# Attention and soft experts in one program: the last key tile in contiguous halves, and a sixth chunk of weights loaded at the first heads

## The chip, the cores and the metric

The kernel runs on one core of one Trainium2 chip. The metric is the device time of one execution in microseconds (us), from its start to its end on that core. The times shown for a kernel are a median over several executions; the profile is of one further execution, whose own time is given beside its span.

## The reference

Two stages, one behind the other. The first is attention within clusters: every query and key goes to the nearest of 16 centroids, and a query sees only the keys of its own cluster.

```python
q_assign = np.argmax(np.einsum('bhsd,hcd->bhsc', q_n, c_n), axis=-1)
k_assign = np.argmax(np.einsum('bhsd,hcd->bhsc', k_n, c_n), axis=-1)
mask = q_assign[:, :, :, None] == k_assign[:, :, None, :]
scores = scale * np.matmul(q, k.transpose(0, 1, 3, 2))
scores = np.where(mask, scores, -1000000000.0)
scores = scores - np.max(scores, axis=-1, keepdims=True)
attn = np.exp(scores)
attn = attn / (np.sum(attn, axis=-1, keepdims=True) + 1e-09)
x = np.matmul(attn, v)        # B=4, H=8, S=768, D=64, float32
```

The second is a soft mixture of 8 experts with 4 slots each over all 3072 rows (4 x 768) of the 512 columns that the heads make together. The dispatch weights are a softmax over the rows, the combine weights one over the 32 slots, of the same logits.

```python
logits = x @ phi                                  # 3072 x 32
d = softmax(logits, axis=0)
slot_input = (d.T @ x).reshape(E, S_per_e, D)     # 8 x 4 x 512
slot_out[e] = np.maximum(slot_input[e] @ w1[e], 0.0) @ w2[e]   # 512 -> 1024 -> 512
c = softmax(logits, axis=1)
out = c @ slot_out                                # 3072 x 512
```

The experts' weights are 16 MB each for `w1` and `w2`, 32 MB together.

## The kernel before

**Heads.** The program goes through 32 heads (4 batches of 8) one after the other, overlapped. A head's queries and keys come transposed from memory in one load (`qkT`, 384 KB), its values in another (`vt`). They are split into a high and a low part for precision (`split_hi`, L601, a cast; `split_lo`, L604, a subtraction on GpSimd); for the first two heads the casts are on ScalarE, then in turn on GpSimd and ScalarE. Copies from SBUF to SBUF (`dma`, L358, from the helpers `place1`, `place2` and so on) put the parts, the one-hot rows of the clusters and the row maxima into the operands of the score matmuls: 96 or 192 KB each, nine or ten for a head. All DMAs go through SyncE's queue. Eight lanes (completion counters) are given to the DMAs in turn: a DMA is issued only when the one eight before it, which had the same lane, is complete.

A head's scores are made twice: `pass_a` (L648) for the row maxima, which VectorE takes (`rowmax`, L656), and `pass_b` (L692), keys by queries, for the exponentials. There are 6 key tiles of 128 keys. For each tile ScalarE makes two exponentials out of PSUM (`expo`, L708), a high part in half precision and the whole in float32; `elow` (L712) subtracts the one from the other for a low part; `pass_c` (L729) multiplies both with the values. A string tells which engine subtracts for each of the 6 tiles, P for GpSimd and D for VectorE (`LOWS`, and `LAST_LOWS` for the last head); with D the whole exponential stays in the PSUM bank of the scores, with P it goes to SBUF. `norm` (L743 to L745) divides by the sums, `xtrans` (L754) and `xtrans_out` (L759) transpose two heads' output together, and `logits` (L766, L778) multiplies with `phi`.

**Order.** `Plan` puts the operations of every engine into one fixed order, from due times in a table `K` and estimated durations. What an engine is to do is therefore a list, and it waits at an instruction whose inputs are not there.

**The last head.** Its last key tile (tile 5) is worked in two halves, u=0 and u=1, so that the first half of the output can be normalised while the second is in work. A half is every second block of 128 queries: `part` takes blocks 0, 2, 4 or 1, 3, 5 of one bank, so that both halves wait for all four matmuls of `pass_b`. Between them stand dummy matmuls without a reader (`fill`, `unread`, L934), 5, 7 and 1 of them about this place.

**Behind the last head.** Dispatch weights (`disp`), their transposes (`dtrans`, L803 and L806), the sum of rows by slot in two parts (`slotin`, L833), their scaling (`fin3`, L914; `fin4`, L918). The combine logits of the last batch are transposed (`comb`, the same lines L803 and L806) after `fin3` of the second part; `comb1` to `comb3` make the softmax. Then the experts: `ffn1` (L1222), `relu`, `ffn1_t` (L1250), `ffn2` (L1264) by three column parts, `sums`, `slots` (L1278), and `combine` (L1298, L1305), whose results leave in ten outputs of 512 KB.

**Weights.** They are 16 chunks of 2 MB: 0 to 7 of `w1`, 8 to 11 and 12 to 15 of `w2`. `NPRE` = 5 chunks have buffers of their own and are loaded in 40 pieces of 256 KB beside the heads from head 2 on (`load_w`, L1149). Seven more go into room that the heads' buffers leave, each piece when its room is free, and four (`used`, `BUF`) into buffers whose weights have been used in the experts.

The program begins with dummy matmuls (`warm`, L1185) that stand between the first real ones. `mask_out` (L584) writes the one-hot mask rows of a head into its operands: for the first half (u=0) of the queries (k=0) and the keys (k=1) on ScalarE, for the other on VectorE; for the second head one call covers all.

## Time and profile before

| | before |
|---|---|
| median of 3 runs | 469.69 us (468.64 to 470.2) |
| the profiled execution | 468.94 us |
| its span in the profile | 465.5 us |
| TensorE busy (PE) | 450.0 us, 97% |
| VectorE busy (DVE) | 365.1 us, 78% |
| ScalarE busy (ACT) | 367.4 us, 79% |
| GpSimd busy (POOL) | 314.2 us, 67% |
| moved by DMA | 103.67 MB, mean 223 GB/s |

Times in the profile count from the start of the span. PE is TensorE's matmuls, PEld its weight loads, SPq the DMA queue of SyncE as its issuing engine. The page cuts the span in 40 slices of 11.6 us; a digit is a busy share in tenths. A line of a timeline has start, duration, engine, line of the kernel, operation, output and inputs by their buffers' names, and in square brackets how long the engine had been idle and what ended that. The chain of waits is followed back from the last instruction, and gives for each moment the work that set the end. In a table of stretches every engine has its busy time in that stretch and its count of instructions; then come TensorE's granted clock (1.00 is full), the mean busy share of the 16 DMA engines and what they moved.

### The profile page before, as it was taken

Reading aid. Unit: us, or ns where it says so; the run is one execution under the profiler, and the core shown is the slowest. Engines: PE = TensorE matmul, PEld = TensorE weight load, DVE = VectorE, ACT = ScalarE, POOL = GpSimd, SP = SyncE. Lnnn points to the kernel's source line nnn. Section 1 sums busy time; section 2 is a strip of 40 time slices with the busy share of each in tenths; the row PEclk is TensorE's granted clock in tenths of the full one; section 3 lists DMA queues with packets and bytes.
Section 4 is the critical chain, followed back from the end, with each engine's and each line's share of the span. In section 5 each row is a group of like instructions: output and inputs, shape, how many; then the busy total and the mean of one; then the engine's idle time right before and its main releaser. Section 6 shows DMA issues by size and latency. Waiting matters only on the chain.

```text
span 465.5 us, 15360 instructions
## 1 busy us (share of the span) xinstructions
PE 450.0 (97%) x6139; PEld 362.5 (78%) x6139; DVE 365.1 (78%) x728; ACT 367.4 (79%) x572; POOL 314.2 (67%) x245
## 2 busy tenths in 40 slices
PE   8999999999999999999999999999999999999993
PEld 7777887979797788888886888787868888753572
DVE  6999898989898889898988888888899875362243
ACT  6379999999998798989895989898969989810042
POOL 8358888888888678787876787878775887501000
PEclk9999999999999999999999999999999999999998
DMA  8945876787777676788676578867854778999997
GB/s 241 227 127 145 223 212 174 213 220 213 188 199 208 177 196 180 195 226 219 186 205 184 143 202 222 222 172 205 222 154 128 203 191 242 341 413 408 408 381 293
DMA packets 43035, 103.67 MB, mean 223 GB/s; under 512 B 7834, under 2 KB 12372, under 8 KB 42964
## 3 DMA queue, kind: packets, MB, share of 16 engines
q1 hardware_dynamic: 42964, 102.69, 75.6%
q8 instruction: 48, 0.79, 0.8%
q14 instruction: 23, 0.19, 0.1%
HBM read 52.63 MB, written 6.29 MB: 127 GB/s over the span
## 4 chain that ended last, share of the span: by engine, by line
PE 88%; DVE 4%; ACT 3%; issue 1%; DMA 1%; POOL 0%; SPq 0%; DVEq 0%; POOLq 0%
PE pb L692 29%; PE pc L729 22%; PE pa L648 16%; PE pso L1264 3%; PE ph L1222 3%; PE pt L483 3%; PE pt L754 2%; ACT w L708 2%; PE pt L766 1%; PE po L1298 1%; PE pt L495 1%; PE pc L1185 1%; PE pt L530 1%; DMA w<-vt 1%; PE pt L667 1%
## 5 line engine op out<-in xcount | busy, mean ns | idle before, releaser
L708 ACT ACTIVATE w<-pb 128x768 f16<-128x768 f32 (+2 forms) x320 | 241.7, 814 | 36.9 <-PE pb L692 34.4
L712 POOL TENSOR_TENSOR w<-w,w 128x768 f16<-128x768 f32 x127 | 209.4, 1657 | 76.7 <-ACT w L708 52.2
L656 DVE TENSOR_REDUCE mc<-pa 128x1 f32<-128x512 f32 (+1 forms) x288 | 188.5, 685 | 28.2 <-PE pa L648 26.5
L692 PE MATMUL pb<-w 128*128 128x512 f32 (+1 forms) x576 | 152.1, 350 | 2.0 <-DVE w L712 1.4
L729 PE MATMUL pc<-vx,w 128*128 128x65 f16 x3402 | 132.0, 194 | 0.6 <-POOL w L712 0.3
L729 PEld LDWEIGHTS <-w 128*128 128x128 f16 x3456 | 116.2, 97 | 13.2 <-issue 8.6
L692 PEld LDWEIGHTS pb<-w 128*128 128x128 f32 x576 | 102.4, 188 | 23.3 <-DVE w L712 4.4
L648 PE MATMUL pa<-w 128*128 128x256 f32 (+1 forms) x384 | 112.8, 368 | 0.4 <-ACT w L584 0.3
L712 DVE TENSOR_TENSOR w<-pb,w 128x768 f16<-128x768 f32 (+1 forms) x66 | 62.0, 940 | 18.1 <-ACT pb L708 14.8
L648 PEld LDWEIGHTS pa<-w 128*128 128x128 f32 x384 | 62.2, 189 | 16.3 <-DVE mc L656 13.0
L604 POOL TENSOR_TENSOR w<-w,w 128x768 fp32r<-128x768 f32 x32 | 58.7, 1834 | 5.4 <-ACT w L601 4.1
L692 PE MATMUL pb<-w,w 128*128 128x512 f32 x192 | 60.3, 337 | 0.0
L708 ACT ACTIVATE pb<-pb 128x768 f32<-128x768 f32 (+1 forms) x66 | 53.6, 812 | 0.0
L692 PEld LDWEIGHTS pb<-w,w 128*128 128x128 f32 x192 | 36.2, 188 | 5.1
L636 POOL TENSOR_TENSOR vx<-w,vx 128x384 f16<-128x384 f32 x32 | 28.7, 895 | 1.2 <-ACT vx L632 1.1
L745 DVE TENSOR_TENSOR w<-pc,z 128x384 f32<-128x384 f32 (+1 forms) x32 | 17.7, 552 | 1.1
L628 ACT ACTIVATE w<-w 128x384 f32<-128x384 f32 x32 | 17.1, 533 | 1.8 <-DMA w<-vt 1.8
L601 POOL CAST w<-w 128x768 fp32r<-128x768 f32 x15 | 12.4, 826 | 8.9 <-DMA w<-w 8.9
L632 ACT CAST vx<-w 128x384 f16<-128x384 f32 x32 | 17.2, 538 | 0.1
L533 ACT ACTIVATE w<-pt,ohsc 128x768 fp32r<-128x768 bf16 x15 | 13.7, 915 | 3.2 <-DVE mc L656 3.2
L754 PE MATMUL pt<-ident,w 128*128 128x128 f32 x90 | 15.8, 285 | 0.0
L1264 PE MATMUL pso<-w,hT 128*32 128x128 f32 (+1 forms) x384 | 15.7, 310 | 0.0
(162 smaller groups left out, 380.2 us busy)
## 6 DMA issues: line engine op xcount, KB each, us to landing
w<-w SPq DMA_DIRECT2D x128, 192.0 KB
w<-w SPq DMA_DIRECT2D x188, 96.0 KB
w<-qkT SPq DMA_DIRECT2D x32, 384.0 KB
w<-w1r SPq DMA_DIRECT2D x40, 256.0 KB
w<-w2b SPq DMA_DIRECT2D x16, 512.0 KB
w<-w2a SPq DMA_DIRECT2D x13, 512.0 KB
w<-vt SPq DMA_DIRECT2D x32, 192.0 KB
out<-w SPq DMA_DIRECT2D x10, 512.0 KB
```

The lines of the kernel that those rows point to most:

```text
L604: nc.gpsimd.tensor_sub(RL[i % 2], R[i % 3], RH[i % 2].bitcast(F32))
L632: (nc.scalar.copy if e == "ACT" else ENG[e].tensor_copy)(VXs[i % 2][:, :, D:2 * D], V[i % 2])
L636: nc.gpsimd.tensor_sub(vx[:, :, 0:D], V[i % 2], vx[:, :, D:2 * D])
L648: nc.tensor.matmul(pa[:, c0:c0 + w], q1[:, q0:q0 + P], k1[:, k0:k0 + w], start=True, stop=True)
L656: nc.vector.tensor_reduce(hd[i]["mc"][:, 4 * m + c0:4 * m + c1], pa.rearrange("p (n c) -> p n c", n=c1 - c0), axis=AX.X, op=ALU.max, negat ...
L692: nc.tensor.matmul(pbt[j % 2][:, q0:q1], k_[:, kc], q_[:, q0:q1], start=(o == 0), stop=(o == 1))
L708: nc.scalar.activation(part(dst, u), part(pbt[j % 2][:, 0:S], u), AF.Exp, scale=SCALE)
L712: (nc.vector if lows(i)[j] == "D" else nc.gpsimd).tensor_tensor(part(EL[n % NEL], u), part(e32(i, j), u), part(EH[n // 2 % (NEH // 2)][:, ...
L729: nc.tensor.matmul(pc[:, c0:c0 + w], e[:, ts], vx[:, j, r0:r0 + w], start=(j == 0 and c0 == 0 and o == 0), stop=(j == NT - 1 and o == 2), ...
L745: nc.vector.tensor_tensor(xn, pv[:, :, :, 0:D], z.unsqueeze(3).to_broadcast([P, 2 if u is None else 1, NU, D]), op=ALU.mult)
L754: nc.tensor.transpose(out=pv[:, a, 0:P] if a < 2 else pv[:, :, P:QS], in_=XN[p % 5][:, u + 2 * a, :], identity=ident)
L1264: nc.tensor.matmul(pso[32 * g:32 * g + 32, 0:w], hT[:, r, ff, g, :], chunk(10 + 2 * q + r if q else 8 + 2 * r + c, (fs * g + f) * w, w), s ...
```

## The change

**A sixth chunk at the first heads.** `NPRE` is 6. The 40 pieces on SyncE's queue still cover chunks 0 to 4, at the same heads; chunk 5 is loaded in four pieces of 512 KB on ScalarE's queue, two behind the key half of `mask_out` of head 0 and two behind that of head 1. Only three chunks (13 to 15) go into used buffers. Room comes from small tiles (`mx`, `m2`, `mc`, `nm`, `z`) that now lie in `siT`, from the mask `em`, now in `acc`, and from a smaller scratch area of the program.

**The last key tile.** `pass_b` of tile 5 is made in two halves, each with two matmuls into a bank of its own. Half 0 is queries 0 to 383 as they lie, with the blocks 0, 2, 4 gathered beforehand in the operand view; on it ScalarE makes one exponential in place, VectorE casts it for the high part and subtracts; on half 1 ScalarE makes two exponentials and VectorE subtracts. The subtraction of tile 4 is moved from GpSimd to VectorE. The dummies are 3, 3 and 1, into another bank. The second transposed copy (`xtrans_out`, u=1) is on ScalarE.

**Combine weights.** The transposes of the last batch's combine logits take the place of 5 dummies before the last part of the dispatch; `comb1` waits for `fin4`. `fin4` of the first part is on ScalarE. In the experts, `ct_rest` comes after the first sums and its copy after `slots`; two calls of `ffn2` are cut at other places, so that the first `combine` stands earlier.

```diff
-LAST_LOWS = "PDPDPD"
+LAST_LOWS = "PDPDDD"
...
-    NPRE = 5
+    NPRE = 6
...
         if u == 0:
             nc.scalar.mul(o, ps, -BIG if k else 1.0)
+            if k == 1:
+                for h in range(2):
+                    load_w(NPRE - 1, (2 * i + h) * CW // 4, CW // 4, nc.scalar)
...
+    def half(u):
+        return pbt[1][:, 512 * u:512 * u + HS].rearrange("p (a c) -> p a c", c=P)
+
+    def pass_b_half(i, j, u):
+        for o, (q_, k_) in enumerate((q1k1(i), q2k2(i))):
+            nc.tensor.matmul(half(u), k_[:, j * P:(j + 1) * P], part(q_, u), start=(o == 0), stop=(o == 1))
...
+    def expo_half(i, j, u):
+        if u == 1:
+            nc.scalar.activation(seg(ehigh(i, j), u), half(u), AF.Exp, scale=SCALE)
+        nc.scalar.activation(half(u), half(u), AF.Exp, scale=SCALE)
+
+    def ehigh_half(i, j, u):
+        nc.vector.tensor_copy(seg(ehigh(i, j), u), half(u))
+
+    def elow_half(i, j, u):
+        nc.vector.tensor_tensor(seg(EL[(NT * i + j) % NEL], u), half(u), seg(ehigh(i, j), u), op=ALU.subtract)
...
-        (nc.scalar.copy if apool(p) is None else nc.vector.tensor_copy)(pr[p]["xT", u], pr[p][u][:, 0:HS])
+        (nc.scalar.copy if apool(p) is None or u == 1 else nc.vector.tensor_copy)(pr[p]["xT", u], pr[p][u][:, 0:HS])
...
         if last:
-            fill("B", 5, [("d4", b)])
+            combs("fill", [("ls", b), ("d4", b), ("ct", 1)])
...
-        nc.vector.tensor_copy(siT[:, ca:cb, :].rearrange("p c s -> p (c s)"), mg["ps", ca][:, 0:(cb - ca) * NS])
+        (nc.vector.tensor_copy if ca else nc.scalar.copy)(
+            siT[:, ca:cb, :].rearrange("p c s -> p (c s)"), mg["ps", ca][:, 0:(cb - ca) * NS])
...
-    em = tail.tile([P, 2, 4, NS], F32, name="em")
+    em = acc[:, 0:2 * 4 * NS].rearrange("p (r g s) -> p r g s", r=2, g=4)
...
-    BUF = list(range(NW)) + [0, 3, 4, 5]
+    BUF = list(range(NW)) + [0, 3, 4]
...
-        m = {0: 12, 3: 13, 4: 14, 5: 15}.get(n)
+        m = {0: 13, 3: 14, 4: 15}.get(n)
```

Below, rows of the order of an engine's instructions: line, operation, output and inputs, and what each waits for (DMAHW with a number is a lane; PE, DVE, Activation and Pool are the other engines). Lines of the changed kernel stand 9 to 51 further down than before.

On ScalarE, from the masks of head 0 to the cast of head 2: L584 is `mask_out` and L601 the cast. Before:

```order
L584 ACTIVATE w_0_88<-pb_124 32x384 [waits PE_49]
L584 ACTIVATE w_0_88<-pb_124 32x384
L490 COPY w_86<-pt 128x384 [waits PE_49]
L584 ACTIVATE w_0_91<-pt 32x768 [waits PE_49]
L584 ACTIVATE w_0_91<-pt 32x768
L601 CAST w_87<-w_86 128x768 [waits DMAHW4_49,DMAHW6_49,DMAHW3_49,DMAHW7_49,DMAHW0_49,Pool_49]
```

In the changed kernel, where they are L593 and L613, and L1197 is `load_w`:

```order
L593 ACTIVATE w_0_89<-pb_122 32x384 [waits PE_49]
L593 ACTIVATE w_0_89<-pb_122 32x384
L1197 DMA w_86<-w1r 128x1024
L1197 DMA w_86<-w1r 128x1024 [waits DMAHW6_49]
L499 COPY w_87<-pt 128x384 [waits PE_49]
L593 ACTIVATE w_0_92<-pt 32x768 [waits PE_49]
L593 ACTIVATE w_0_92<-pt 32x768
L1197 DMA w_86<-w1r 128x1024 [waits DMAHW4_49]
L1197 DMA w_86<-w1r 128x1024 [waits DMAHW6_49]
L613 CAST w_88<-w_87 128x768 [waits DMAHW1_49,DMAHW7_49,DMAHW0_49,Pool_49]
```

The four loads stand behind the masks of heads 0 and 1. They have the lanes 3, 6, 4 and 6; the second waits for an earlier copy of lane 6, the fourth for the second load.

On SyncE's queue, from the values of a head (`vt`) over the place copies of head 1 (`w_0_91`) to those of head 2 (`w_1_92`, `w_1_89`). Before:

```order
L475 DMA w_94<-vt 128x384 [waits DMAHW0_49,Pool_49]
L358 DMA w_0_91<-w_87 64x768 [waits DMAHW1_49]
L358 DMA w_0_91<-w_87 64x768 [waits DMAHW2_49]
L475 DMA w_94<-vt 128x384 [waits DMAHW3_49,Pool_49]
L358 DMA w_0_91<-w_87 32x768 [waits DMAHW4_49]
L358 DMA w_0_91<-w_87 32x768 [waits DMAHW5_49]
L472 DMA w_86<-qkT 128x768 [waits DMAHW6_49,PE_49]
L358 DMA w_1_92<-w_87 64x768 [waits DMAHW7_49]
L358 DMA w_1_89<-w_87 64x768 [waits DMAHW0_49,Activation_49]
L358 DMA w_1_89<-w_87 64x768 [waits DMAHW1_49]
L358 DMA w_1_89<-w_87 32x768 [waits DMAHW2_49]
L358 DMA w_1_89<-w_87 32x768 [waits DMAHW3_49,Pool_49]
```

In the changed kernel, where L367 is the copy and the operands are `w_0_92`, `w_1_93` and `w_1_90`:

```order
L484 DMA w_95<-vt 128x384 [waits DMAHW2_49,Pool_49]
L367 DMA w_0_92<-w_88 64x768 [waits DMAHW3_49]
L367 DMA w_0_92<-w_88 64x768 [waits DMAHW5_49]
L484 DMA w_95<-vt 128x384 [waits DMAHW7_49,Pool_49]
L367 DMA w_0_92<-w_88 32x768 [waits DMAHW0_49]
L367 DMA w_0_92<-w_88 32x768 [waits DMAHW1_49]
L481 DMA w_87<-qkT 128x768 [waits DMAHW2_49,PE_49]
L367 DMA w_1_93<-w_88 64x768 [waits DMAHW3_49]
L367 DMA w_1_90<-w_88 64x768 [waits DMAHW4_49,Activation_49]
L367 DMA w_1_90<-w_88 64x768 [waits DMAHW5_49]
L367 DMA w_1_90<-w_88 32x768 [waits DMAHW6_49]
L367 DMA w_1_90<-w_88 32x768 [waits DMAHW7_49,Pool_49]
```

The rows are the same and in the same order; the lanes are others. The first place copy of head 1 now waits for lane 3, that of the first load, and two copies of head 2 for lanes 4 and 6, those of the third and the fourth.

On VectorE, the last subtractions of the last head (L712) and the start of the normalisation. Before:

```order
L712 TENSOR_TENSOR w_95<-pb_125,w_95 128x768 [waits PE_49,Activation_49,Pool_49]
L712 TENSOR_TENSOR w_95<-pb_125,w_95 128x3x128 [waits PE_49,Activation_49]
L712 TENSOR_TENSOR w_95<-pb_125,w_95 128x3x128
L743 TENSOR_SCALAR z<-pc 128x3 [waits PE_49]
L744 RECIPROCAL z<-z 128x3 [waits DVE_49]
L745 TENSOR_TENSOR w_96<-pc,z 128x3x64 [waits DVE_49]
```

In the changed kernel, where L733 is a whole subtraction, L746 the cast of the first half and L749 the subtraction of a half:

```order
L733 TENSOR_TENSOR w_96<-pb_123,w_96 128x768 [waits PE_49,Activation_49,Pool_49]
L733 TENSOR_TENSOR w_96<-pb_122,w_96 128x768 [waits PE_49,Activation_49,Pool_49]
L746 CAST w_96<-pb_123 128x384 [waits Activation_49]
L749 TENSOR_TENSOR w_96<-pb_123,w_96 128x384 [waits DVE_49,PE_49]
L749 TENSOR_TENSOR w_96<-pb_123,w_96 128x384 [waits PE_49]
L778 TENSOR_SCALAR siT<-pc 128x3 [waits PE_49]
L779 RECIPROCAL siT<-siT 128x3 [waits DVE_49]
L780 TENSOR_TENSOR w_97<-pc,siT 128x3x64 [waits DVE_49]
```

Tile 4's subtraction and the cast are new on VectorE. Of the subtractions of the two halves, before as now, the second has no wait for ScalarE of its own.

On TensorE, from the sums by group of the dispatch (L891) to the first expert matmul (L1222). Before, without the five dummies (L934, each with its weight load) that stand where the line of dots is:

```order
L891 MATMUL pa_126<-fw,w_96 128x4
L803 MATMUL pa_127<-ident,dT 128x2x64
L806 MATMUL pa_127<-ident,dT 64x2x32 x2
...
L904 MATMUL pa_126<-fw,w_96 128x1
L833 MATMUL pb_124<-w_96,dn 32x256 x8
L833 MATMUL pb_125<-w_96,dn 32x128 x16
L914 MATMUL pa_127<-stk_71,acc 128x32 x2
L914 MATMUL pa_126<-stk_71,acc 128x32 x2
L803 MATMUL pt<-ident,ls 128x2x64
L806 MATMUL pt<-ident,ls 64x2x32 x2
L1222 MATMUL ph<-w_81,siT 32x512 x8
```

In the changed kernel (L838 and L841 are the transposes of L803 and L806, L1273 is the expert matmul):

```order
L926 MATMUL pa_124<-fw,w_97 128x4
L838 MATMUL pa_125<-ident,dT 128x2x64
L841 MATMUL pa_125<-ident,dT 64x2x32 x2
L838 MATMUL pt<-ident,ls 128x2x64
L841 MATMUL pt<-ident,ls 64x2x32 x2
L939 MATMUL pa_124<-fw,w_97 128x1
L868 MATMUL pb_122<-w_97,dn 32x256 x8
L868 MATMUL pb_123<-w_97,dn 32x128 x16
L949 MATMUL pa_125<-stk_71,acc 128x32 x2
L949 MATMUL pa_124<-stk_71,acc 128x32 x2
L1273 MATMUL ph<-w_81,siT 32x512 x8
```

The transposes of `ls` moved from before the experts to where the dummies were.

## Rows read from the trace of the kernel before

**Rows 1.** From the page: the span, the busy time of TensorE, and the clock granted to it in the 40 slices.

```profile
span 465.5 us, 15360 instructions
...
PE 450.0 (97%) x6139; PEld 362.5 (78%) x6139; DVE 365.1 (78%) x728; ACT 367.4 (79%) x572; POOL 314.2 (67%) x245
...
PEclk9999999999999999999999999999999999999998
```

**Rows 2.** The table of stretches: from and to, length; then busy time and instructions of TensorE, its weight loads, VectorE, ScalarE and GpSimd; granted clock, mean share of the 16 DMA engines, GB/s.

```profile
12.00:14.00 2.00, 1.54 (x17) 1.02 (x15) 1.90 (x7) 0.00 (x0) 2.00 (x2) 1.00 1.06 216
24.00:26.00 2.00, 1.87 (x12) 1.28 (x10) 1.84 (x4) 0.93 (x3) 0.00 (x0) 1.00 1.06 262
26.00:28.00 2.00, 2.00 (x16) 1.24 (x15) 1.89 (x3) 2.00 (x4) 0.00 (x0) 1.00 0.71 183
28.00:28.50 0.50, 0.50 (x6) 0.27 (x2) 0.50 (x2) 0.50 (x2) 0.32 (x1) 1.00 0.00 0
40.00:340.00 300.00, 298.52 (x4083) 248.17 (x4079) 261.73 (x509) 273.97 (x422) 239.77 (x162) 1.00 0.73 198
430.00:444.00 14.00, 14.00 (x240) 8.19 (x236) 2.41 (x4) 1.34 (x3) 0.00 (x0) 1.00 1.03 408
446.00:458.00 12.00, 11.33 (x290) 9.10 (x286) 6.24 (x13) 4.87 (x11) 0.00 (x0) 1.00 0.99 385
458.00:459.00 1.00, 0.00 (x0) 0.00 (x0) 1.00 (x3) 0.88 (x3) 0.00 (x0) 1.00 0.66 252
459.00:460.00 1.00, 0.00 (x0) 0.00 (x0) 0.25 (x1) 0.00 (x0) 0.00 (x0) 1.00 1.03 410
462.00:463.00 1.00, 0.00 (x0) 0.00 (x0) 0.00 (x0) 0.00 (x0) 0.00 (x0) 0.50 0.94 346
```

**Rows 3.** Timeline of ScalarE at the first heads: the masks of head 0 (L584, 32x384), those of head 1 (L584, 32x768), and the first and last lines behind them.

```profile
10.60 0.97 ACT L584 ACTIVATE w<-pb 32x384 fp32r<-32x384 bf16 x2
14.42 0.48 ACT L490 COPY w<-pt 128x384 f32<-128x384 f32 x1 [2.85 <-PE pt L483]
15.71 1.61 ACT L584 ACTIVATE w<-pt 32x768 fp32r<-32x768 bf16 x2 [0.81 <-PE pt L576]
...
19.70 0.52 ACT L628 ACTIVATE w<-w 128x384 f32<-128x384 f32 x1 [1.10 <-DMA w<-vt]
```

**Rows 4.** Timeline of SyncE's queue: the issues of the place copies of head 1.

```profile
12.55 1.14 SPq L358 DMA_DIRECT2D w<-w  x2
...
14.57 1.18 SPq L358 DMA_DIRECT2D w<-w  x2
```

**Rows 5.** Timeline of GpSimd: its first cast (L601) and the low parts of the first key tiles that it subtracts (L712).

```profile
28.18 0.83 POOL L601 CAST w<-w 128x768 fp32r<-128x768 f32 x1 [8.11 <-DMA w<-w]
28.97 1.66 POOL L712 TENSOR_TENSOR w<-w,w 128x768 f16<-128x768 f32 x1
...
32.43 1.66 POOL L712 TENSOR_TENSOR w<-w,w 128x768 f16<-128x768 f32 x1
```

**Rows 6.** The chain of waits at head 1: dummies (L1185) and the first scores (L648).

```profile
19.43 1.34 PE pc L1185 x12
20.77 0.71 PE pa L648 x3
```

**Rows 7.** Timeline of TensorE: the first scores of head 2 (L648) and the products with the values (L729) of the first key tiles.

```profile
29.93 0.40 PE L648 MATMUL pa<-w 128*128 128x256 f32 x2
...
30.51 1.40 PE L729 MATMUL pc<-vx,w 128*128 128x65 f16 x36
...
34.45 0.72 PE L729 MATMUL pc<-vx,w 128*128 128x65 f16 x18
```

**Rows 8.** The chain of waits from the last key tile to the first expert matmul: start, duration, engine, output, line.

```profile
403.69 0.98 PE pb L692 x4
...
404.69 0.49 ACT w L708
...
406.08 0.39 ACT pb L708
...
406.50 1.02 DVE w L712 x2
...
407.54 0.17 DVE z L743
...
412.46 0.39 PE pb L934 x5
...
416.88 0.14 PE pt L803
417.02 0.27 PE pt L806 x4
417.29 4.84 PE ph L1222 x41
```

**Rows 9.** Timelines of ScalarE and VectorE at the last key tile, and the two transposed copies (L759).

```profile
405.08 0.49 ACT L708 ACTIVATE pb<-pb 128x384 f32<-128x384 f32 x1
405.60 0.49 ACT L708 ACTIVATE w<-pb 128x384 f16<-128x384 f32 x1
...
406.50 1.02 DVE L712 TENSOR_TENSOR w<-pb,w 128x384 f16<-128x384 f32 x2 [2.87 <-ACT pb L708]
...
408.95 1.23 DVE L759 COPY xT<-pa 128x384 f32<-128x384 f32 x2
```

More of the change, by code (lines that the diff above doesn't have):

```diff
@@ L236, in clustered_attention_then_soft_moe, with take @@
     siT = const.tile([P, NCC, NS], F32, name="siT")
-    NPRE = 5
+    small = siT.rearrange("p c s -> p (c s)")
+    SMALL = dict(mx=(0, 24, 1), m2=(24, 24, 1), mc=(48, 12, 2), nm=(72, 6, 2), z=(84, 6, 2))
+    taken = dict.fromkeys(SMALL, 0)
+    def take(k, w=None):
+        c0, n, bufs = SMALL[k]
+        c0 += taken[k] % bufs * n
+        taken[k] += 1
+        return small[:, c0:c0 + (w or n)]
+    NPRE = 6
     CW = 4 * FF
@@ L504, in assign1 @@
         pv = pview(p)
-        mx = wk1.tile([P, NG], F32, name="mx")
+        mx = take("mx")
         nc.vector.tensor_reduce(mx, pv, axis=AX.X, op=ALU.max)
@@ L512, in assign2 @@
         nc.vector.tensor_tensor(pv, pv, desc.unsqueeze(1).to_broadcast([P, NG, NCL]), op=ALU.mult)
-        m2 = pr[p]["m2"] = wk1.tile([P, NG], F32, name="m2")
+        m2 = pr[p]["m2"] = take("m2")
         nc.vector.tensor_reduce(m2, pv, axis=AX.X, op=ALU.max)
@@ L551, in assign_1 @@
         pv, G = aview(i), 2 * NT
-        mx = wk1.tile([P, NG], F32, name="mx")[:, 0:G]
+        mx = take("mx", G)
         nc.vector.tensor_reduce(mx, pv, axis=AX.X, op=ALU.max)
@@ L558, in assign_2 @@
         nc.vector.tensor_tensor(pv, pv, desc.unsqueeze(1).to_broadcast([P, G, NCL]), op=ALU.mult)
[L559 removed]
+        m2 = hd[i]["m2"] = take("m2", G)
         nc.vector.tensor_reduce(m2, pv, axis=AX.X, op=ALU.max)
@@ L653, in rowmax @@
         if "mc" not in hd[i]:
-            hd[i]["mc"] = wk2.tile([P, 2 * NT], F32, name="mc")
+            hd[i]["mc"] = take("mc")
         c0, c1 = ((0, 1), (1, 3), (3, 4))[n]
@@ L660, in negmax @@
     def negmax(i):
-        nm = hd[i]["nm"] = wk2.tile([P, NT], F32, name="nmx")
+        nm = hd[i]["nm"] = take("nm")
         nc.vector.tensor_reduce(nm, hd[i]["mc"].rearrange("p (t n) -> p t n", n=2),
@@ L736, in norm @@
         xn = XN[(i // 2) % 5][:, :, h * D:(h + 1) * D].rearrange("p (a u) d -> p u a d", u=2)
-        z = wk2.tile([P, 2, NU], F32, name="z")
+        z = take("z").rearrange("p (u a) -> p u a", u=2)
         if u is None:
@@ L1256, in ffn1_t, with ffn2 @@
                 op=ALU.mult)
-    def ffn2(pso, q, r, c=None, half=None):
+    def ffn2(pso, q, r, c=None, half=None, f0=None, f1=None):
         w = PART[q][1]
         fs = NFC // 2 if q == 0 else NFC
-        for f in range(fs) if half is None else range(half * fs // 2, (half + 1) * fs // 2):
+        if half is not None:
+            f0, f1 = half * fs // 2, (half + 1) * fs // 2
+        for f in range(f0 or 0, f1 or fs):
             ff = f if q else c * fs + f
```

106 lines of the change are left out of this document (60 added, 46 removed).

## The prediction

> **What bounds the kernel now.** I read the page first, for the share of each engine and for the strip of slices; then one table of stretches; then the timelines of the engines that issue or await copies at the first heads; last the chain of waits at the last head. On the page TensorE is busy 450.0 of 465.5 us, and its clock row is full to the last slice [rows 1]. The table of stretches sharpens this: between 40 and 340 us TensorE works 298.52 of 300 us [rows 2]. So there is no slack to win there, and, what matters here, none in which lost time could be caught up: a delay of TensorE before 40 us arrives at the end in full, if nothing later shrinks. The profiled execution took 468.94 us for a span of 465.5; the median of the runs shown, 469.69, is 0.75 above it. I make the sum against 468.94 and add 0.75 at the end.
>
> The copies tell another story. At 12 to 14 us and at 24 to 26 us all 16 DMA engines are busy (share 1.06 both times) although they move only 216 and 262 GB/s; from 26 to 28 the share is 0.71, and from 28.0 on nothing is moved [rows 2]. The copies of the first three heads thus come as one stream that is never interrupted and ends just before 28.2 us, where GpSimd's first cast has waited 8.11 us for a copy [rows 5]. This is the one place before the tail where DMA time sets the pace.
>
> **Part 1: a sixth chunk at the first heads.** Four loads of 512 KB, 2.10 MB in all, join that stream. ScalarE issues them behind its two mask activations, which end at 11.57 (10.60 + 0.97) and 17.32 (15.71 + 1.61) [rows 3]. Issuing them costs ScalarE little: the first pair is followed by a wait of 2.85 us, and of the second pair's delay 1.10 us is covered by the wait before 19.70 [rows 3]; if that cover were gone, the vt activation behind it would be late by the issue time, and SyncE's rows show 0.57 us for one (1.14 for two) [rows 4].
>
> What costs is engine time. While this kernel streams weights alone (430 to 444 us) 16 engines at share 1.03 move 408 GB/s [rows 2]; at that rate 2.10 MB take 5.14 us of all 16. Nothing in the stream leaves a gap for them before 26 us, and the 0.29 of two microseconds that is free after it (0.6 us) is the stream's own thin end, where the copies wait for each other. The lanes decide who goes first: in the new order SyncE's first place copy of head 1 waits for the lane on which the first load went, and two copies of head 2 wait for the lanes of the third and the fourth. So all four loads are done before the last copy of head 2 even starts; they cannot be put off into the idle time behind 28.0. I take 5.14 us later for the end of the stream: 28.18 becomes 33.3.
>
> Who waits for it? On GpSimd the cast at 28.18 stands before the first low part (28.97, 1.66 us to 30.63) [rows 5]; TensorE's product with that tile is the second half of the 36 matmuls from 30.51, so wanted at about 31.2 (30.51 + 0.70 of 1.40) [rows 7]. Slack 0.6. TensorE's scores of head 2 start at 29.93 [rows 7], 1.4 after the copies' end at 28.5 at the latest. The next low part ends at 34.09 (32.43 + 1.66) and is used at 34.45: slack 0.4 [rows 5, 7], less than the 0.6, but within what this estimate can tell. By the scores the delay is 5.14 - 1.4 = 3.7, by GpSimd's chain 5.14 - 0.6 = 4.5. TensorE takes its work in order, so the larger counts: +4.5. Earlier, at 20.77, TensorE starts the scores of head 1, with 1.34 us of dummy matmuls before them [rows 6]; the place copies issued from 12.55 and 14.57 [rows 4] will land some 2.6 us later (half of the 2 MB is ahead of them). That stall is not added: it moves TensorE's own part later and is contained in the 4.5.
>
> Bounds. No row shows loads from HBM beside copies inside SBUF on two queues. Below: if the two kinds overlap in the engines, the cost can go to nothing. Above: at the rate of the mixed stretch (230 GB/s, between the 216 and 262 of [rows 2]) 2.10 MB take 9.1 us, and the delay is 9.1 - 0.6 = 8.5. I take 4.5, from the row in which the same kind of load runs alone.
>
> On this the Trainium skill has a rule ("DMA: Bandwidth & Descriptors", section "Issuing engines are not separate DMA queues"): transfers begun by ScalarE, SyncE or GpSimd run on the same 16 engines and interleave, and a second issuer only saves issue time. By that rule the loads get no bandwidth of their own and the delay stands; if ScalarE's queue were a separate path, the sum would be 4.5 us less. The shares of 1.03 and 1.06, which leave no room [rows 2], agree with the rule, but no row has two busy queues.
>
> **Part 2: less to load late.** From 430 to 444 us TensorE works 14.00 of 14.00 us beside the stream of weights [rows 2]: it does not wait for them. What follows is outputs: the engines are full from 446 to 458 (share 0.99), have a thin microsecond at 458 (0.66), and are full again behind the last copies (1.03 at 459, 0.94 still at 462) [rows 2]. So the last group of outputs goes at the engines' pace once it is there, and it is there when TensorE's last combine is done. 2 MB less before can only take away what is queued ahead of that group; the thin microsecond says that this is little. Gain 0.3, bounds 0 and 1.5 (the time by which the last stretch can shrink if nothing at all is ahead).
>
> **Part 3: the last key tile.** Before: four matmuls from 403.69, exps from 404.69 to 406.47, both subtractions together from 406.50 to 407.52, the normalisation at 407.54 [rows 8]. Now three exps instead of four, and a cast on VectorE instead. Whether the halves come apart is told by the waits. Before, the first half's exps were done at 405.57 (405.08 + 0.49), yet VectorE began at 406.50, released by ScalarE's last [rows 9]: its one wait covered both halves. In the new order it is the same: the cast waits for ScalarE, the second subtraction, which reads ScalarE's second half, has no such wait of its own, so the cast's wait holds for all three exps; and the second exp waits for no matmul, so the first one's wait covers both halves of the scores. Thus ScalarE starts at 404.69 as before, its second piece follows after 0.52 (a piece that waits for the one before: 405.08 to 405.60), the third 0.39 later, and it ends at 404.69 + 0.52 + 0.39 + 0.49 = 406.1. VectorE then casts (between the 0.51 of a half subtraction and the 0.62 of a copy of 384 columns, half of the 1.23 at 408.95 [rows 9]; I take 0.5) and subtracts twice, 1.02, with some 0.1 for waiting on its own cast: 407.7. That is 0.2 later than 407.52. If the halves do come apart, the cast lies beside ScalarE's second half and VectorE is through at 406.6: 0.9 earlier. Tile 4's subtraction, now VectorE's, falls into VectorE's idle 2.87 us before 406.50 [rows 9] and costs nothing. The second transposed copy on ScalarE beside the first on VectorE gains 0.1.
>
> **Part 4: the combine weights.** Their transposes (0.14 and 0.27 us from 416.88) stand directly before the first expert matmul at 417.29 [rows 8]; now they take the place of the 0.39 us of dummies at 412.46 [rows 8], while TensorE waited anyway. The experts' first matmul then waits for ScalarE's copy of the first part alone, which is done before. Gain 0.4.
>
> The renamed small tiles, the zeros of the experts' mask and the order of the tail leave TensorE there the same instructions, back to back; VectorE's and GpSimd's idle time covers the rest.
>
> **Sum.** 468.94 + 4.5 + 0.2 - 0.1 - 0.4 - 0.3 = 472.84; with 0.75 for the runs, 473.6 us.
>
> **Rivals.** *The loads slip in, and the tail wins (0.14).* Loads from HBM and copies within SBUF overlap, so that head 2's last copy lands by 28.18 + 0.6, which is the point that decides; and the queue of outputs, free of 2 MB, gives the whole 1.5. For it: 216 GB/s at the same share as 408, so engines that count as busy may be waiting. Against: the lanes put the loads ahead of head 2's copies. 468.94 - 0.4 - 1.5 = 467.0, as shown 467.8: faster than before.
> *They slip in, no more (0.10).* Without the delay the sum is 468.34, as shown 469.1: no difference.
> *Half an overlap (0.14).* The stream ends 2.6 us later, the delay is 2.0: 470.3, as shown 471.1.
> *The loads at the mixed rate (0.12).* 8.5 in place of 4.5: 476.8, as shown 477.6. For it: both busy stretches shown lie near 230 GB/s [rows 2].
> *The halves come apart (0.04).* 0.9 earlier instead of 0.2 later: 471.7, as shown 472.5. Against it: the waits above.
> The forecast has 0.46.
>
> **How the numbers follow.** A measurement of this kernel tells 0.3% from no change: 468.28 and 471.10 are the bounds. Faster: the first rival, 0.14. Same: the second and the third (at the upper bound), 0.24. Slower: the other cases, 0.62. The range goes from 468.0, which cuts off half of the first rival, to 476.8, short of the mixed rate's time by part of its spread; the likeliest case alone has 472.0 to 475.0.
>
> **What would show it.** In the changed profile: DMA traffic without a gap at 28 us, and a gap near 33; GpSimd's first cast at about 33.3 with a wait of some 13 us instead of 8.11; TensorE idle for some 2 us before 23.5 and again between 31 and 36, and from 40 us the same instructions about 4.5 later. At the last tile VectorE's cast begins after ScalarE's third exp. From the last scores to the first expert matmul 13.3 us instead of 13.6 (403.69 to 417.29 [rows 8]). The forecast is wrong if GpSimd's cast comes before 29.5, or if TensorE's clock falls in the early stalls: before, it is full at every slice but the last [rows 1].

## The result and the profile after

The changed kernel takes 475.63 us (median of 6, 472.68 to 479.33), the kernel before 469.43 (6 runs, 468.64 to 470.20). The ratio is 1.0128, with a 95% interval of 1.0093 to 1.0162: slower by 6.2 us. Slower was forecast, and 475.63 lies in the range (468.0 to 476.8), 2.0 above the forecast of 473.6 and 2.0 below the 477.6 of the rival with the mixed rate. Not forecast was the spread: 6.7 us, where the kernel before has 1.6 here and 3.7 over 23 runs beside a later experiment.

The profiled execution took 475.47 us for a span of 473.7. From the page after (the last row: queue, packets, MB, share of 16 engines):

```profile
span 473.7 us, 15338 instructions
...
PE 453.2 (96%) x6128; PEld 365.6 (77%) x6128; DVE 366.2 (77%) x728; ACT 367.6 (78%) x573; POOL 312.8 (66%) x244
...
PEclk9989999999999999999999999999999999999997
...
q10 hardware_dynamic: 576, 2.10, 1.4%
```

TensorE has 453.2 us of work instead of 450.0 [rows 1], the clock row has an 8 in its third slice, and q10 is ScalarE's queue with its 2.10 MB. The stretches of the first heads, columns as in [rows 2]:

```profile
22.00:24.00 2.00, 1.20 (x11) 1.01 (x10) 1.90 (x4) 0.00 (x0) 0.50 (x1) 1.00 0.99 315
...
26.00:28.00 2.00, 0.00 (x0) 0.00 (x0) 0.00 (x0) 0.52 (x1) 0.00 (x0) 1.00 1.06 235
28.00:30.00 2.00, 1.62 (x6) 1.55 (x7) 0.38 (x1) 0.00 (x0) 0.00 (x0) 0.56 0.80 172
30.00:32.00 2.00, 2.00 (x14) 1.82 (x13) 1.51 (x5) 0.00 (x0) 0.00 (x0) 0.59 0.93 255
...
34.00:36.00 2.00, 2.00 (x11) 1.53 (x11) 1.83 (x4) 1.19 (x2) 0.00 (x0) 1.00 0.51 117
36.00:38.00 2.00, 2.00 (x16) 1.06 (x15) 1.98 (x4) 2.00 (x4) 1.00 (x2) 1.00 0.00 0
```

TensorE stands still from 23.2 to 28.4 us, and then works at a granted clock of 0.56 and 0.59, that is for the most part at the lower of its levels, before it is full again. The DMA engines are busy through all of it (share 0.99 to 1.06 in the rows up to 28 us, 0.80 and 0.93 to 32); the empty stretch that lay at 28 us [rows 2] now lies at 36. The chain of waits says what stood in between:

```profile
12.19 5.03 DMA w<-w1r
...
17.24 0.50 SPq L367
...
18.47 1.12 SPq L484
...
19.64 8.27 DMA w<-w
...
28.38 1.20 PE pa L660 x3
29.58 2.13 PE pc L1236 x10
```

The first load lands at 17.22 (12.19 + 5.03), and only then SyncE issues head 1's first place copies (at 12.55 in [rows 4]). Its last two, issued from 19.64, take 8.27 us to land, at 27.9, and with them head 1's scores begin at 28.38 (20.77 in [rows 6], where head 0's scores had begun 2.0 us earlier than here). Here is why they take so long; ScalarE's issues beside the mask of head 1 (L593), and its wait for a vt load:

```profile
12.19 0.88 ACTq L1197 DMA_DIRECT2D w<-w1r  x2
...
18.13 0.80 ACT L593 ACTIVATE w<-pt 32x768 fp32r<-32x768 bf16 x1 [0.81 <-PE pt L585]
18.14 1.45 ACTq L1197 DMA_DIRECT2D w<-w1r  x2
...
26.77 0.52 ACT L640 ACTIVATE w<-w 128x384 f32<-128x384 f32 x1 [5.75 <-DMA w<-vt]
```

The third and fourth load were issued from 18.14, before those copies, and share the engines with them. They went out as the first mask of head 1 began (18.13), not when the second ended (19.74), as the prediction had taken it. Had SyncE not been held until 17.24, the copies would have been ahead of them: without the first pair of loads they go out from 15.70 (e8, below). The sum of SyncE's waits for the loads from 8 to 40 us (total, times, longest):

```profile
SPq L367 <- DMA w<-w1r: 8.0, 3, 3.7
```

The last of the three ends at 27.65, when the copy of head 2 with the fourth load's lane goes out; that one the prediction had read from the order. GpSimd, for [rows 5]:

```profile
36.14 0.82 POOL L613 CAST w<-w 128x768 fp32r<-128x768 f32 x1 [13.64 <-DMA w<-w]
37.83 1.66 POOL L733 TENSOR_TENSOR w<-w,w 128x768 f16<-128x768 f32 x1 [0.86 <-ACT w L730]
```

Its cast is late as forecast (36.14 after a wait of 13.64 us; 33.3 had been said, which is 35.3 if the start of head 0's scores, 2.0 us later here, is taken off), but the low part behind it then waits 0.86 us for ScalarE: GpSimd is not what is late last.

At the other end, for [rows 8]:

```profile
412.83 0.98 PE pb L713 x4
...
413.83 0.48 ACT pb L743
...
414.40 0.49 ACT w L742
414.89 0.39 ACT pb L743
...
415.31 0.57 DVE w L746
...
415.97 1.02 DVE w L749 x2
...
417.01 0.17 DVE siT L778
...
421.84 0.26 PE pt L838
422.10 0.27 PE pt L841 x4
...
425.83 0.63 PE pa L949 x4
```

ScalarE's three exps run to 415.28, the cast begins at 415.31 behind the last of them, both subtractions end at 416.99, and the normalisation starts 4.18 us behind the first scores (3.85 in [rows 8]). The combine transposes stand at 421.84, and nothing lies between the last `fin3` (425.83 + 0.63) and the expert matmuls at 426.46.

### The profile page after: what moved, and what is told of

The parts are those of the page before. It is cut to its first block, busy times and chain, and to the rows that moved or that the text cites. A ratio compares the mean times of both kernels' runs of the same rounds, so it can differ in the third digit from the quotient of the medians.

```text
span 473.7 us, 15338 instructions
## 1 busy us (share of the span) xinstructions
PE 453.2 (96%) x6128; PEld 365.6 (77%) x6128; DVE 366.2 (77%) x728; ACT 367.6 (78%) x573; POOL 312.8 (66%) x244
## 4 chain that ended last, share of the span: by engine, by line
PE 87%; DVE 4%; DMA 3%; ACT 2%; issue 2%; SPq 0%; POOL 0%; DVEq 0%; POOLq 0%; ACTq 0%
PE pb L704 28%; PE pc L764 21%; PE pa L660 15%; PE pso L1317 3%; PE ph L1273 3%; PE pt L492 2%; PE pt L789 2%; DMA w<-w 2%; PE pc L1236 2%; ACT w L730 1%; PE pt L801 1%; DMA w<-w1r 1%; PE pt L539 1%; PE pt L504 1%; PE po L1351 1%
## 5 line engine op out<-in xcount | busy, mean ns | idle before, releaser
L730 ACT ACTIVATE w<-pb 128x768 f16<-128x768 f32 (+1 forms) x317 | 240.1, 816 | 36.4 <-PE pb L704 32.3
L733 POOL TENSOR_TENSOR w<-w,w 128x768 f16<-128x768 f32 x126 | 208.0, 1659 | 76.2 <-ACT w L730 52.2
L668 DVE TENSOR_REDUCE siT<-pa 128x1 f32<-128x512 f32 (+1 forms) x288 | 188.6, 685 | 34.4 <-PE pa L660 32.8
L704 PE MATMUL pb<-w 128*128 128x256 f32 (+1 forms) x572 | 151.5, 351 | 1.9 <-DVE w L733 1.3
L733 DVE TENSOR_TENSOR w<-pb,w 128x768 f16<-128x768 f32 x65 | 61.9, 952 | 15.5 <-ACT pb L730 12.1
L730 ACT ACTIVATE pb<-pb 128x768 f32<-128x768 f32 x65 | 53.4, 822 | 0.0
L648 POOL TENSOR_TENSOR vx<-w,vx 128x384 f16<-128x384 f32 x32 | 28.8, 899 | 1.1 <-ACT vx L644 1.1
L613 POOL CAST w<-w 128x768 fp32r<-128x768 f32 x15 | 12.4, 826 | 14.3 <-DMA w<-w 14.3
L780 DVE TENSOR_TENSOR w<-pc,siT 128x384 f32<-128x384 f32 (+1 forms) x32 | 17.6, 551 | 1.1
L1236 PE MATMUL pc<-ident 128*128 128x128 f32 x76 | 14.5, 346 | 1.4 <-POOL ident masks.py:199 1.4
```

The source lines that it names most:

```text
L648: nc.gpsimd.tensor_sub(vx[:, :, 0:D], V[i % 2], vx[:, :, D:2 * D])
L668: nc.vector.tensor_reduce(hd[i]["mc"][:, 4 * m + c0:4 * m + c1], pa.rearrange("p (n c) -> p n c", n=c1 - c0), axis=AX.X, op=ALU.max, negat ...
L704: nc.tensor.matmul(pbt[j % 2][:, q0:q1], k_[:, kc], q_[:, q0:q1], start=(o == 0), stop=(o == 1))
L730: nc.scalar.activation(dst, pbt[j % 2][:, 0:S], AF.Exp, scale=SCALE)
L733: (nc.vector if lows(i)[j] == "D" else nc.gpsimd).tensor_tensor(EL[(NT * i + j) % NEL], e32(i, j), ehigh(i, j), op=ALU.subtract)
L780: nc.vector.tensor_tensor(xn, pv[:, :, :, 0:D], z.unsqueeze(3).to_broadcast([P, 2 if u is None else 1, NU, D]), op=ALU.mult)
```

## The experiments

The first profile of the kernel before is a lucky reference: the last section shows that its TensorE came to full rate early. So all profiles are compared from the first scores of head 0 on, and a second profile of the unchanged kernel was taken. In this table, read from the timelines: the start of the scores of head 1 and of head 2 and of the last key tile's scores, all from the start of head 0's scores; then from the last tile's scores to the normalisation, on to the first expert matmul, and on to TensorE's last matmul.

```
us                          head 1  head 2   last tile  norm  experts  end of PE
before (rows above)           9.15   18.31    392.07    3.85    9.68    40.47
before, second profile        9.37   18.65    392.39    3.85    9.67    40.46
changed                      14.78   25.27    399.23    4.18    9.38    39.93
changed, second profile      13.43   24.96    398.90    4.17    9.38    39.93
later on ScalarE (e2)         9.37   18.67    393.35    4.19    9.39    39.92
same place, SyncE (e3)       10.59   26.38    400.35    4.19    9.39    39.92
29 more dummies (e4)         15.83   25.00    398.87    4.19    9.39    39.93
17 more dummies (e12)        17.52   28.08    402.11    4.20    9.39    39.93
behind SyncE's pieces (e6)    9.36   18.65    393.92    4.19    9.39    39.92
head 1's pair only (e8)       9.36   19.00    394.41    4.19    9.38    39.92
head 0's pair only (e9)       9.77   20.22    394.63    4.18    9.39    39.92
late parts only (e10)         9.35   18.65    393.29    4.20    9.39    40.06
two pairs of banks (e11)      9.35   18.67    392.42    3.30    9.39    40.42
```

**e5, the kernel before once more.**

> The kernel before, unchanged, for a second profile: in the first one TensorE's first scores began at 11.6 us, in every profile since at 13.6 to 14.6, with the 12 transposes ahead of them taking 1.52 us there and 2.77 here. Theory (TensorE reaches its full rate at another time after the start from one execution to the next, whatever the kernel): 11.6 or 13.6 to 14.6, either is possible, and from there to the scores of head 2 again 18.3 us. Rival (the changed kernels start slower by their code): 11.6 again.

One run of 469.92 us, its first scores at 14.38. The way on to head 2 is 18.65, and GpSimd's first cast comes at 30.43, 16.05 behind the first scores (16.56 in the first profile). The late start belongs to no kernel. In this execution the copies are not the uninterrupted stream that the prediction had read from [rows 2]; the share of the engines falls to a half (1.05 in the first profile) and rises again before the stream ends:

```profile
22.00:24.00 2.00, 2.00 (x19) 1.95 (x19) 1.90 (x4) 0.23 (x1) 1.29 (x1) 1.00 0.50 106
```

**e13, the changed kernel once more.** It was to tell what separates its runs at 472.7 us from those at 475.5 and more; expected for one of the latter was a lower clock and 10 us or more from head 1 to head 2. Two runs, 475.84 (the profiled one) and 476.87 us: the way is 11.53 us, at the clock shown with e12 below. No run near 472.7 came up, so the other half of the question stays open. What differs from the first profile of the changed kernel is the order of issue: the first of head 1's last two copies went out 0.17 us ahead of the third load, and took 7.39 us all the same.

```profile
18.96 7.39 DMA w<-w
```

```profile
19.13 0.84 ACTq L1197 DMA_DIRECT2D w<-w1r  x2
```

So a copy need not stand behind the loads to be late; it is enough that they are in the engines with it. Head 1 is late by 4.1 us here instead of 5.4, and GpSimd's cast by 5.0 (21.04 behind the first scores) instead of 6.5.

**e2, the four loads later on the same queue.** Out of `mask_out`, into `expo`:

```diff
+        if i == 0 and j in (0, 3):
+            for h in range(2):
+                load_w(NPRE - 1, (2 * (j // 3) + h) * CW // 4, CW // 4, nc.scalar)
```

> The same four loads of 512 KB on ScalarE's queue, but issued later, two behind each of two pairs of exponentials of head 0, when the copies of head 2 are through and the DMA engines were idle before the change (28 to 33 us). Theory (it is the time of the loads that costs, not the second queue): 468 to 469.5, GpSimd's first cast near 28.2. Rival (a second queue disturbs SyncE's copies wherever it stands, by lanes and by interleaving): 471 or more, with a stall of TensorE within 10 us behind the issue.

469.69 us (10 runs), ratio 0.9994 (0.9976 to 1.0012): the loss is gone with the place, at the same bytes, size and queue. Head 2 is where it was. Not all is free: a later head's load of queries and keys, issued behind the four, now needs 7.84 us,

```profile
34.63 7.84 DMA w<-qkT
```

and from head 2 to head 3 the run loses 1.1 us against the second profile of before.

**e3, the same place on SyncE's queue.** `eng=nc.sync` for the four loads.

> The same four loads at the same place of the program, issued by SyncE instead of ScalarE, so that one queue holds all. Theory (2.1 MB of engine time ahead of the place copies): GpSimd's first cast at about 33.3 to 34 (28.2 and 5.1 us), TensorE late by 4.5 to 5.5 at 45 us, median 472 to 473. If the cast comes at 36 as with ScalarE's queue, the second queue has no part in the loss. Rival (two queues at once are served worse than one): clearly below the changed kernel, and runs that agree within 1.5 us where those of the changed kernel spread over 6.6.

477.42 us (4 runs, 472.64 to 478.43), ratio 1.0143 (1.0077 to 1.0210). One queue is no better than two, and its runs spread as much, so the rival falls. The delay only moves: head 1 is late by 1.2 us, head 2 by 7.7. In its chain:

```profile
11.33 8.72 DMA w<-w1r
...
20.07 4.73 DMA w<-w
...
26.84 9.93 DMA w<-qkT
```

The first load, among the copies, needs 8.72 us and lands at 20.05, and a load of queries behind the second pair needs 9.93 us. TensorE stands still for it, and its clock falls here too (0.63 and 0.52 from 36 to 40 us). My number was too small as well: GpSimd's cast comes 23.9 us behind the first scores, 7.9 later than in the second profile of before, not 5.1.

**e9 and e8, one pair each.** `if k == 1 and i == 0:` and `if k == 1 and i == 1:`; the other half of the chunk goes behind every tenth of SyncE's pieces.

> The other half: ScalarE loads two of the four pieces, behind the masks of head 0; the rest in four pieces on SyncE's queue as in the run with head 1. Theory (head 1's first place copy waits for the lane of the first load and all of head 1's copies stand behind 1.05 MB): the scores of head 1 late by 3 to 5 us, head 2 as late, median 472 to 474. Rival (bytes ahead of head 2's copies): the same 3 to 3.5 us at head 2 as with the loads behind head 1, and the scores of head 1 late by less.

> ScalarE loads only two of the four pieces, behind the masks of head 1; the other half of the chunk goes in four pieces of 256 KB on SyncE's queue behind every tenth of the 40. Theory (the time is set by the copies of head 1, which stood behind the first two loads): the scores of head 1 near 9.3 us after those of head 0 as without early loads, the scores of head 2 late by 1 to 2.5 us (1.05 MB at 300 GB/s are 3.5 us, less a slack of 1.4 to 1.75), median 470 to 472. Rival (what counts is the copies of head 2, that is the bytes ahead of them, wherever they stand): late by about half of the loss, 3 to 3.5, as with the loads behind head 0.

472.38 us (ratio 1.0063, 1.0037 to 1.0089) with head 0's pair, 471.33 (1.0051, 1.0026 to 1.0076) with head 1's. The medians fall where they were expected, the stages do not. With head 0's pair SyncE is held just as long, its place copies go out at

```profile
17.09 1.14 SPq L367 DMA_DIRECT2D w<-w  x2
...
19.86 1.18 SPq L367 DMA_DIRECT2D w<-w  x2
```

and yet head 1 is late by 0.4 us, not by 3 to 5, since these copies now land within 4 us, the last at 23.2. With head 1's pair they go out before the loads, as without them, and head 2 is late by 0.35 us, not by 1 to 2.5:

```profile
15.70 1.18 SPq L367 DMA_DIRECT2D w<-w  x2
```

At head 2's scores the pairs cost 1.6 and 0.35 us, by the normalisation of head 0 2.0 and 1.3; both together cost 6.6 at either place. (The profile of the run with head 0's pair is of one of its two fastest, 470.70 us, so these numbers are rather low for it.) What is late last in both is the path that the prediction had priced, GpSimd's cast and first low part; with head 0's pair:

```profile
28.62 3.87 DMA w<-w
...
33.28 1.66 POOL w L733
34.99 1.22 PE pc L764 x34
```

The cast comes 2.8 and 2.1 us later than in the second profile of before, and all but 0.8 of it reaches the normalisation.

So neither the hold by the lane alone nor half the bytes alone makes the loss. With both pairs the first holds SyncE by the lane until the second goes out, head 1's last copies are in the engines together with it, and TensorE stands still until its clock falls. e3 shows that this is not the only way to such a loss: there nothing overtakes, and head 2 is late by 7.7 us. No run has the loads with other lanes, so what the lane costs by itself is not shown. (Further on the run with head 1's pair loses another 1.0 us, 0.8 of it at head 15, the other 0.2. That SyncE's extra pieces do it is not shown: e10, which has none, loses 0.96 at one place.)

**e4 and e12, more dummies before the scores of head 1.** One number in the list of `warms` is 30, or 18, instead of 1.

> The changed kernel with 29 more dummy matmuls (about 3.2 us of TensorE at full clock) just before the scores of head 1, where TensorE was idle from 23.2 to 28.4 us and its clock then fell to half for some 4 us. Theory (the fall of the clock costs 1.3 us of the loss, as the same pieces took 5.4 instead of 4.1 us): granted clock 1.00 from 28 to 32 us, the way from the scores of head 1 to the first scores of the next pass back to 4.1 us, median 1 to 1.5 us below the changed kernel. Rival (the dummies only push the scores back): the scores of head 1 start later than the last copy they wait for by more than 0.5 us, time as the changed kernel or above.

477.14 us (4 runs): not faster, as the rival had it. The clock did stay up while TensorE was kept busy, as these stretches show,

```profile
28.00:30.00 2.00, 2.00 (x21) 2.00 (x20) 0.00 (x0) 0.00 (x0) 0.00 (x0) 1.00 0.84 181
30.00:32.00 2.00, 2.00 (x19) 1.96 (x18) 0.80 (x2) 0.00 (x0) 0.00 (x0) 1.00 0.77 209
```

and from head 1 to head 2 it took 9.17 us again, instead of 10.49 in the changed kernel; the ten dummies behind head 1's first scores take 1.11 us, where they took 2.13 above. But the added dummies ended 2.3 us behind the last copy, as I had mis-sized them (one entry of the list is two matmuls of 0.11 us, 0.22 and not 0.11), and that ate the gain.

> The changed kernel with 17 more dummies before the scores of head 1 instead of 29; one takes 0.22 us, so 3.7 us in place of 6.4, to end about when the copies of head 1 land (near 28 us). Theory (the fall of the clock costs 1.3 us): clock full, scores of head 1 at the time of the changed kernel within 0.5 us, scores of head 2 9.2 us behind them instead of 10.5, median 0.8 to 1.5 us below the changed kernel's 475.6. Rival (head 2's own copies set the time as well, so what head 1 gains is lost again there): scores of head 2 within 0.5 us of the changed kernel's.

476.16 us (4 runs). In this execution the first scores came early (11.32), so the dummies ended at 24.5, TensorE was idle until 28.84, and the clock fell all the same (0.74 at 28 to 30, 0.50 at 30 to 32 us): 10.56 us to head 2. The run tests nothing it was made for; whether a better number of dummies would give a net gain stays open. In the second profile of the changed kernel (e13) the fall comes earlier and costs more, 11.53 us from head 1 to head 2:

```profile
26.00:28.00 2.00, 0.00 (x0) 0.01 (x1) 0.00 (x0) 0.00 (x0) 0.00 (x0) 0.72 0.88 224
28.00:30.00 2.00, 1.98 (x8) 1.90 (x9) 0.75 (x2) 0.00 (x0) 0.00 (x0) 0.50 0.52 138
```

**e1 and e6, the sixth chunk on SyncE's queue beside the heads.** e1 plans 48 pieces instead of 40; e6 keeps the plan and adds to every fifth piece one of chunk 5:

```diff
+        if q % 5 == 4:
+            load_w(NPRE - 1, (0 + q // 5) * CW // 8, CW // 8)
```

> The sixth chunk is not loaded by ScalarE at the first heads but in 8 more pieces of 256 KB on SyncE's queue beside the heads from the second on, as the other five; all else as changed. Theory (the loads at the first heads delay the place copies of heads 1 and 2, all of the loss is there, and what comes behind the last key tile gains about 1 us): the scores of head 1 start near 20.8 us and GpSimd's first cast near 28.2 as before, median 468 to 469, spread below 1.5 us. Rival (the loss comes from the small tiles in one buffer or from the order at the end): 473 to 476, with the first heads as before the change.

> The changed kernel without ScalarE's loads; the sixth chunk goes in 8 pieces of 256 KB on SyncE's queue, each directly behind every fifth of the 40 pieces that are there, so that no other instruction moves against the changed kernel. Theory (the loss was the place of the loads, and what comes behind the last key tile gains about 1 us): 468 to 469.3. Rival (SyncE's queue has no room for 8 more issues beside the heads, as the run with 48 pieces in a new order, 538 us, may show): above 472, with waits of TensorE for copies between heads 8 and 31.

e1 took 537.96 us (ratio 1.1468), with all first heads as before the change: the 68 us are lost from head 8 on. In e1 the pieces stand at other heads and a few of GpSimd's and ScalarE's instructions in another order; SyncE's copies then wait 44.9 us in all for `pass_b` (21.2 before), and `pass_b` reads what they bring; which piece begins it was not tried. e6 took 470.11 us (10 runs), ratio 1.0020 (0.9993 to 1.0047): no difference that can be told, with 1.8 us lost between the normalisations of heads 14 and 24 against the second profile of before. As e6 keeps the small tiles in one buffer and the order at the end, e1's loss is in neither of them, against the rival of e1.

**e10, the late parts without the sixth chunk.** `NPRE = 5` and the four late chunks as before.

> The changed kernel without the sixth chunk (five chunks ahead, four late, as before the change); what is new behind the last key tile stays, and the small tiles in one buffer too. Theory (the halves lose 0.2 to 0.4 us, the combine transposes win 0.3 to 0.4, the tail about 0.5 of which the outputs keep nothing): from the last scores to the normalisation 4.2 us as in the changed kernel (before 3.85), to the first expert matmul 13.6 as before, time 0 to 0.7 us below the kernel before. Rival (the changed end is worth the 1 us that its wording of halves would give): 1.2 us or more below.

469.31 us (12 runs), ratio 0.9988 (0.9968 to 1.0007). The pieces behind the last tile are as in the changed kernel: 0.35 us lost to the normalisation, 0.28 won to the experts, 0.4 in the tail. Its last tile comes 0.9 later than in the second profile of before, though it has no early load: about head 21 one copy comes late, and TensorE waits 0.68 us for it. Differences of some 1 us between head 2 and the last tile can therefore be chance, in the other rows of the table too.

**e11, the halves in two pairs of banks.**

```diff
-LAST_LOWS = "PDPDDD"
+LAST_LOWS = "PDPDPD"
...
-        return pbt[1][:, 512 * u:512 * u + HS].rearrange("p (a c) -> p a c", c=P)
+        return pbt[1 - u][:, 0:HS].rearrange("p (a c) -> p a c", c=P)
```

> As the run with the late parts only, with two edits at the last key tile: the second half of the scores goes into the other pair of PSUM banks instead of the second bank of the same pair, and tile 4's subtraction goes back to GpSimd so that this pair is free. In its order the cast waits for the first half's exponential alone. Theory (one buffer for both halves joined their waits; that is why the halves do not come apart): VectorE casts while ScalarE works on the second half, from the last scores to the normalisation 2.8 to 3.1 us instead of 4.2, time 1 to 2 us below the kernel before. Rival (VectorE is the bound there anyway, or GpSimd's tile 4 ends last): 3.7 us or more, and no difference to the run with the late parts only.

The halves come apart. The cast starts 1.17 us behind the tile's first scores (2.48 in the changed kernel), while ScalarE works on the second half:

```profile
408.11 0.56 DVE L743 CAST w<-pb 128x384 f16<-128x384 f32 x1 [1.22 <-ACT pb L740]
...
408.42 0.49 ACT L740 ACTIVATE pb<-pb 128x384 f32<-128x384 f32 x1
```

The normalisation comes after 3.30 us, not 4.18; 2.8 to 3.1 had been expected. It could be earlier still, but now GpSimd's tile 4 is what ends last, TensorE waits for it:

```profile
409.10 0.20 PE L761 MATMUL pc<-vx,w 128*128 128x65 f16 x1 [0.36 <-POOL w L730]
```

In time it makes no difference, where 1 to 2 us had been expected: 469.49 us (12 runs), ratio 0.9997 (0.9978 to 1.0016). What the last tile wins, 0.55 us against the kernel before, is too little for this measurement. So no version tried beats the kernel before beyond doubt.

## Why the prediction was right, and where its steps failed

**The sum.** Forecast +3.9 us on the profile's time; measured +6.2 in the medians. By the table (changed against the second profile of before) it is +6.84 to the last tile, +0.33 to the normalisation, -0.29 to the experts, -0.53 in the tail: +6.35.

**Part 1, the direction: right.** The loads ahead of the copies cost time that is carried to the end (6.6 us at head 2, 6.8 at head 31's last tile). e2 shows that it is the place: the same loads on the same queue, later, lose nothing that can be told. The rule of the Trainium skill that I had weighed ("DMA: Bandwidth & Descriptors", section "Issuing engines are not separate DMA queues") agrees with e3: one issuer or two, about the same loss (ratios 1.0143 and 1.0128).

**Part 1, the size: the term 4.5 was mis-sized, it is 6.6 (6.3 in e13).** The step that failed is "That stall is not added ... and is contained in the 4.5". The copies of head 1, not head 2's, set the time: head 1 was late by 5.4 us (4.1 in e13), not 2.6, as lane 3 held SyncE and the last copies were in the engines together with loads three and four. I had the lane's wait in the order before me and read from it only that the loads cannot be put off; I did not follow which of ScalarE's later issues go out meanwhile. TensorE stood still once, for 5.2 us, where two stalls had been forecast.
The clock, which I had only named as what would make the forecast wrong, fell, and made the way from head 1 to head 2 10.49 instead of 9.28 us: 1.2 of the 6.6 (11.53, or 2.3 of the 6.3, in e13). e4 shows this part by its opposite. By its own sign, then, the forecast had the mechanism wrong at this point, although the time lies in its range.
The path that was priced, GpSimd's, was not far off. Its cast, told from the first scores, moved by 6.5 us where 5.14 had been said (22.54, against 16.05), by 5.0 in e13 and by 7.9 on one queue. For 2.10 MB that is 320, 420 and 270 GB/s, from no slower than the weights alone to near my upper bound. Less the 0.8 us that e9 and e8 show, it would give 4.2 to 5.7 us in the changed kernel, about the 4.5; but another path ended later. That the number came as near as it did is in part luck.

**Part 1, the slack.** 0.6 us by GpSimd was read from one execution, and it holds: 0.8 in e9 and e8. What the first profile could not show is the gap in the stream that the second one has. It may be why half the bytes moved the cast by only 2.8 and 2.1 us (370 and 500 GB/s); no run shows that by itself.

**Rivals.** That the loads slip in fell with the result. The mixed rate (477.6) is as near to the measured 475.63 as the forecast, and its delay of 8.5 is nearer to e3's 7.7 than my 4.5. (In the first rival's sum the 0.1 of the last tile is left out; with it, 467.1 instead of 467.0.) "The halves come apart" fell, for the reason given, and e11 shows that one buffer for both was the reason.

**Part 2.** Forecast 0.3; the table shows 0.53 to TensorE's end, and the outputs' end is 7.38 behind that instead of 7.35 (7.1 to 8.1 in the other profiles). Right in size, and not in its words: I looked for the gain in the queue of outputs, and it came in TensorE's part of the tail. What gave it is not told apart: every run of the table with the sixth chunk has 0.53 or 0.54, e10 without it 0.40, and e11, also without it and with the same order of the tail, 0.04.

**Part 3: right.** Forecast 0.2 later, measured 0.33: the cast took 0.57 where I took 0.5, and VectorE began 0.07 later.

**Part 4 and the second copy.** Forecast 0.5 together, measured 0.29. The transposes take 0.53 us in their new place (421.84 to 422.37), where 0.39 of dummies stood, so 0.1 of the gain is given back.

## What to carry to other kernels

Before a transfer is put early "into free time", look for the stretch in which the engines move nothing, and put it there: the same 2.1 MB on the same queue cost 6.6 us at 12 to 20 us and about 1 at 30. A transfer on a second queue takes a completion lane from the first; follow which instruction then waits, and what is in the engines with it when it goes. A path that is priced right gives the time only if no other path ends later: price the stalls that "are contained" too. Two halves of a tile are two only when their buffers are; the order of waits shows it before any run.

## What the runs showed that was not expected

TensorE's rate at the start differs from one execution to another, at a granted clock that the profile gives as 1.00. The twelve transposes and the next twenty dummies, first in the first profile of before, then in the changed kernel:

```profile
5.30 1.52 PE L541 MATMUL pt<-w 128*128 128x32 f32 x12 [0.42 <-DVE w L355]
6.66 2.48 PE L1185 MATMUL pc<-ident 128*128 128x128 f32 x20
```

```profile
5.17 2.77 PE L550 MATMUL pt<-w 128*128 128x32 f32 x12 [0.24 <-DVE w L364]
7.75 4.10 PE L1236 MATMUL pc<-ident 128*128 128x128 f32 x20
```

The transposes are the same instructions and take 1.52 or 2.77 us. In all later profiles but one, of any kernel, the first scores came at 13.3 to 14.6 us, in e12 at 11.3. The first profiled execution differs in another way too: its time exceeds its span by 3.44 us, where most runs have 1.8. So the 0.75 that I added was not a property of the kernel, and a single profile is no reference to better than some 2 us at its start.

ScalarE's DMA issues did not wait for the activations ahead of them. In e12 the first pair went out 0.54 us before the masks began behind which it stands in the order:

```profile
9.76 0.91 ACTq L1197 DMA_DIRECT2D w<-w1r  x2
10.30 0.97 ACT L593 ACTIVATE w<-pb 32x384 fp32r<-32x384 bf16 x2
```

The changed kernel's runs lie apart by up to 6.7 us. Its two runs at 472.7 have a mean clock of 0.996, the other four, 475.5 to 479.3, have 0.981 to 0.994. The two are 3.3 us above the kernel before, near the 3.9 of the forecast, which has no fall of the clock in it; the four are 6.0 to 9.9 above. A profile of one of the two was not caught, so that the clock is the whole of this spread is not shown.
